# Scoring the second token tile beside the first, with constants and the first tile loaded first

## The chip, the cores and the metric

The kernel runs on one core of a Trainium2 chip. The metric is the device time of one execution in microseconds (us); lower is better. Engines: PE (TensorE, matrix products), DVE (VectorE), ACT (ScalarE), POOL (GpSimd, here the issuer of the gathers), SP (SyncE, the issuer of the plain loads and stores), and 16 DMA engines that move the data of both issuers.

## What is computed

An input of 2048 tokens of width 448 is normed; the result is the input plus two branches that both read the norm.

```python
x = A_q
xn = _layernorm(x, axis=-1)
return x + _A_ref(xn, A_k, A_v, A_shift_k, A_ssm_k, A_ssm_D) + _B_ref(xn, B_w_q, B_k1, B_k2, B_u, B_v)
```

Branch A is a short convolution of k (4 taps), times v, then a causal convolution of length 2048 for each channel (by Fourier transforms), times the normed input. Branch B picks experts:

```python
q = jnp.einsum("nd,dhc->nhc", xf, w_q)          # 16 heads, 2 x 256
s1 = jnp.einsum("nhd,ed->nhe", q1, k1)          # 64 keys; s2 likewise
i1 = jnp.argsort(-s1, axis=-1)[..., :K]         # K = 2; i2 likewise
...
top_e = jnp.take_along_axis(eidx, ord2, axis=-1)   # 2 of the 4 pairs
g = _softmax(top_s, axis=-1)
act = _gelu(jnp.einsum("nd,nhkd->nhk", xf, u[top_e]))
out = jnp.einsum("nhk,nhk,nhkd->nd", g, act, v[top_e])
```

So each token reads 32 rows of u and 32 of v, and which rows is known only after scoring.

## The kernel before

**Tiles.** The tokens are 16 tiles of 128. `XA` holds all of them (loaded by `load_x`, normed in place by `norm`).

**Weights and scores.** `weights(h)`, for each of the 16 heads: SP loads 896 KB of w_q into one of four buffers (`wqb`); PE multiplies it with the keys (`pw`, L415); ACT copies the product (L418); PE turns it (`pt`, L424); ACT and DVE split it into a high and a low part (L431 to L437) in `WR`. A load waits until the product that read its buffer has run. `turn(T)` turns a token tile on PE and splits it into `xh` (ACT) and `xl` (DVE). `score(T, n)` makes the scores of four heads (11 matmuls, L477 to L481), then DVE finds maxima (L486) and their places (L493). `pick` selects the experts of these heads on DVE and ACT, spreads them over partitions by a product (`place`, L556), and ACT writes `idx` and `gat` (L562), eight slots of tiles. Tile 0 is scored and picked in turns of four heads while the weights come in; tile 1 by itself once they are all there, with one `pick` for its 16 heads; later tiles in pairs.

**Experts.** A tile has eight batches (128 in all), a batch four gathers on POOL (L586), each of 128 rows of u and v side by side (448 KB), into a ring of five batches. At most six gathers are on their way (`OUTSTANDING`). A gather needs the `idx` of its two batches' four heads. Then DVE multiplies with the spread token tile (L619), ACT sums (L625), POOL (from batch 104 on DVE) forms the coefficients (L632, L633), and PE adds up the values in `pv` (L638). `fold` takes the tile out. Where PE would sit idle inside a tile it runs small filling products (L1094).

**Convolution.** In two parts of 28 and 84 groups of channels: `conv_first` (in0, in1; loads `kvh`, taps L703, first transform L720), `conv_mid` (sp0, sp1; L767 to L817), `conv_last` (out0, out1; turning L858, copy to `zt` L860, last product L865, gate L876). All work in areas of one tile `S1`; before, out0's `zt` has a tile of its own. in1 needs the space of the scoring's tiles, so `switch` frees these after the last tile is scored and out0 is done; its first loads and taps work in `S1` and need not wait for that.

**Order.** Nothing runs in the order of the source. Each operation is given to a planner (`Plan.solve`) with a duration and a key; the planner walks through modelled time and takes, on each engine, the ready operation with the smallest key. `nb` is the earliest planned time. The engines then run the planned sequence in order, whatever the true times; a late load therefore holds all that was planned behind its user on that engine. `RANK` adds to the keys of each kind of operation a correction, given at four points and interpolated between. Plain loads leave SP in the order of their keys: before, kk, two heads' weights, x0, two more heads, c1 (the identity and other constants), then x1, x2 to 3, x4 to 9, x10 to 15 and the weights of the other heads. `join` makes later writers of an area wait for earlier users.

## Time and profile before

| | us |
|---|---|
| median of 3 runs | 909.22 (908.57 to 912.37) |
| the profiled execution | 899.54 |
| its span, first to last instruction | 897.6 |
| weights of the last head turned (last L425 on PE) | 70.3 |
| last score (L481) | 499.6 |
| first and last gather issued | 41.6, 871.5 |

The profiled execution is 9.7 us shorter than the median; all times of the trace belong to it. Busy time of an engine says little here by itself: the stages have different limits, and what counts is which wait ends last in each.

### The profile page before, as it was taken

The page shows a single profiled execution, that of the slowest core. Times are in us where ns is not written, and L with a number is a line of the kernel's source. Part 1 is how long each engine was busy: PE and PEld are TensorE (multiplying, and loading weights), DVE is VectorE, ACT ScalarE, POOL GpSimd, SP SyncE. Part 2 cuts the span into 40 slices and gives each one's busy share as a digit, 9 for nine tenths or more (in the row PEclk, how much of TensorE's full clock was granted, in tenths as well). Part 3 has the DMA queues.
Part 4 walks back from the last instruction along what each step waited for, and adds up shares of the span by engine and source line. Part 5 has one row for each costly group of instructions (what it writes and reads, how often), then busy time and mean ns, then how long its engine had stood idle before and what let it go on. Part 6 is the DMA issues. An engine that isn't in the chain of part 4 may idle for free.

```text
span 897.6 us, 15165 instructions
## 1 busy us (share of the span) xinstructions
PE 734.1 (82%) x4696; PEld 465.9 (52%) x4696; DVE 673.5 (75%) x1570; ACT 568.2 (63%) x1874; POOL 593.5 (66%) x740
## 2 busy tenths in 40 slices
PE   5988988898888889888797878787688887778776
PEld 2436756556555565556465645465343443345554
DVE  3568988887787878787887867758798897864454
ACT  2598664557565766566663675537798887764562
POOL 0157587886777767776777677757877776665550
PEclk9899999998999989998998989999999999997797
DMA  9898798888989999898889899988999999999885
GB/s 372 345 398 296 229 309 304 294 284 301 313 314 318 304 314 311 309 332 297 297 293 344 294 309 343 356 326 295 354 318 325 319 328 313 309 309 336 299 299 143
DMA packets 62586, 279.47 MB, mean 311 GB/s; under 512 B 14112, under 2 KB 23584, under 8 KB 62240
## 3 DMA queue, kind: packets, MB, share of 16 engines
q0 software_dynamic: 40960, 234.91, 75.2%
q1 hardware_dynamic: 21536, 43.49, 13.7%
q8 instruction: 39, 0.64, 0.3%
q14 instruction: 51, 0.42, 0.1%
HBM read 272.29 MB, written 6.08 MB: 310 GB/s over the span
## 4 chain that ended last, share of the span: by engine, by line
PE 49%; ACT 12%; issue 12%; DVE 9%; DMA 7%; POOL 7%; another core or an unknown queue 3%; DVEq 0%; POOLq 0%; SPq 0%; ACTq 0%
PE pv L638 9%; ACT ring L625 6%; POOL ring L586 5%; PE bank L477 4%; PE bank L720 4%; PE bank L478 3%; PE bank L479 3%; PE bank L814 3%; PE pv L1094 3%; PE bank L771 3%; DMA ring<-in_uv_dram,idx 3%; PE bank L865 2%; DVE ring L619 2%; DMA S<-in_kvh_dram 2%
## 5 line engine op out<-in xcount | busy, mean ns | idle before, releaser
L586 POOL DMA_INDIRECT ring<-in_uv_dram,idx x512 | 509.3, 995 | 270.6 <-issue 91.3
L625 ACT ACTIVATE ring<-ring 128x448 f32<-128x448 f32 x512 | 288.4, 567 | 49.8 <-DVE ring L619 30.5
L619 DVE TENSOR_TENSOR ring<-ring,xs 128x1792 f32<-128x1792 f32 x128 | 256.9, 2014 | 54.7 <-DMA ring<-in_uv_dram,idx 37.6
L638 PE MATMUL pv<-ring,cc 128*32 128x448 f32 x1024 | 136.4, 604 | 67.3 <-issue 36.5
L486 DVE MAX8 SC<-bank 128x8 f32<-128x64 f32 x512 | 118.5, 232 | 37.2 <-PE bank L481 10.0
L625 ACT ACTIVATION_READ_ACCUMULATOR ring<-ring 128x1 f32 x512 | 97.0, 189 | 0.0
L1094 PEld LDWEIGHTS pv<-c 128*128 128x128 f32 x596 | 80.3, 201 | 26.6 <-issue 25.5
L477 PE MATMUL bank<-WR,xh 128*128 128x512 f32 x192 | 84.4, 440 | 2.7 <-ACT R L724 1.0
L720 PE MATMUL bank<-c,S 128*64 128x132 f32 x896 | 68.1, 295 | 22.1 <-issue 7.0
L1094 PE MATMUL pv<-c 128*128 128x64 f32 x596 | 85.6, 285 | 0.0
L478 PE MATMUL bank<-WR,xh 128*128 128x512 f32 x192 | 78.1, 407 | 0.0
L638 PEld LDWEIGHTS pv<-ring,cc 128*32 128x32 f32 x1024 | 21.3, 112 | 108.3 <-issue 65.0
L479 PE MATMUL bank<-WR,xl 128*128 128x512 f32 x192 | 77.3, 403 | 0.0
L720 PEld LDWEIGHTS bank<-c,S 128*64 128x64 f32 x896 | 53.1, 143 | 45.3 <-issue 12.5
L771 PE MATMUL bank<-x1b,S 128*128 128x336 f32 x132 | 51.6, 505 | 10.8 <-DVE x1b L839 7.0
L724 ACT ACTIVATE x1b<-bank 128x264 f32<-128x264 f32 x84 | 30.8, 387 | 40.0 <-PE bank L720 29.7
L788 DVE TENSOR_TENSOR S<-bank,S 128x224 f32<-128x224 f32 (+1 forms) x66 | 40.5, 620 | 18.6 <-ACT S L782 13.4
L703 DVE TENSOR_TENSOR S<-S 128x1024 f32<-128x1024 f32 x28 | 34.9, 1245 | 25.7 <-PE bank L720 11.5
L493 DVE FIND_INDEX8 SC<-SC,bank 128x8 uint32<-128x256 f32 x128 | 52.5, 423 | 0.0
L477 PEld LDWEIGHTS bank<-WR,xh 128*128 128x128 f32 x192 | 37.9, 197 | 26.6 <-issue 11.5
L782 ACT ACTIVATE S<-bank 64x112 f32<-64x112 f32 x132 | 33.9, 257 | 21.8 <-PE bank L767 13.0
L632 POOL TENSOR_TENSOR cc<-sm,c 128x128 f32<-128x128 f32 x104 | 46.0, 442 | 2.2
(142 smaller groups left out, 1090.8 us busy)
## 6 DMA issues: line engine op xcount, KB each, us to landing
R<-in_wq_dram SPq DMA_DIRECT2D x16, 896.0 KB
S<-in_kvh_dram SPq DMA_DIRECT2D x28, 400.0 KB
ring<-in_uv_dram,idx POOLq DMA_INDIRECT x512
S<-in_fq_dram SPq DMA_DIRECT2D x32, 128.0 KB
XA<-in_x_dram SPq DMA_DIRECT2D x2, 1344.0 KB
out_dram<-fo SPq DMA_DIRECT2D x12, 224.0 KB
x1b<-out_dram SPq DMA_DIRECT2D x9, 224.0 KB
out_dram<-XA SPq DMA_DIRECT2D x2, 840.0 KB
```

The lines of the kernel that those rows point to most:

```text
L477: nc.tensor.matmul(o, xh[:, c, :], wh[:, c, ns], start=(c == 0), stop=False)
L478: nc.tensor.matmul(o, xh[:, c, :], wl[:, c, ns], start=False, stop=False)
L479: nc.tensor.matmul(o, xl[:, c, :], wh[:, c, ns], start=False, stop=False)
L486: nc.vector.max(mx[:, 8 * n + j, :] if safe else m2[:, m, 2 * j:2 * j + 8], bank[s.i][:, 64 * j:64 * j + 64])
L493: nc.vector.max_index(m4i[:, 2 * m + g, :], m2[:, m, 8 * g:8 * g + 8], bank[s.i][:, 256 * g:256 * g + 256])
L586: g = nc.gpsimd.indirect_dma_start(dst, None, uv, bass.IndirectOffsetOnAxis(ap=idx[:, T % 8, r, j:j + 1], axis=0)).ins
L619: op("DVE", dve(m * D), lambda: nc.vector.tensor_mul(U[:, :m, :], U[:, :m, :], xs[:, :m, :D]), r=["xs"], w=u[:m], key=k, name="prod")
L625: op("ACT", 0.575, lambda r=r: nc.scalar.activation(U[:, r, :], U[:, r, :], AF.Copy, accum_out=aw[:, r:r + 1]), w=[u[r], ("aw", b % 4, r)] ...
L638: v = nc.tensor.matmul(pv[32 * r:32 * r + 32, :D], cc[b % 3][:, r, :], ring[:, b % RING, r, D:], start=(j == 0), stop=(j == NB - 1), tile_ ...
L720: nc.tensor.matmul(o[64 * i:64 * i + 64, w * j:w * j + w], src, f1[:, i, :], start=True, stop=True, tile_position=(0, 64 * i))
L771: op("PE", 0.95 * n / 448 + 0.05, lambda t=t, sl=sl: nc.tensor.matmul(bank[sl.i][:, :n], fm, x1[p][:, :, q, t, :], start=True, stop=True), ...
L1094: nc.tensor.matmul(pv[:, D:], ident, c1[:, P:P + 512 - D], start=False, stop=False)
```

## The change

The scores of tile 1 are made four heads at a time, right after tile 0's of the same heads; its 16 heads are still picked at once, after tile 0's last. Tile 1's load, norm and turning move into the weights' loop at head 2. `xh` and `xl` exist twice, by the tile's parity. The loads of x4 to 15 get a name of their own and an earliest planned time of 14 and 26 us; c1 and x0 are loaded ahead of the weights by their keys. For the space, `zt` goes: out0 uses a part of `S1` (where in1's taps stand), a third buffer for part 1's spectra lies in `Y`, and the scratch of the dynamic DMAs is halved. in1's first users of `S1` now wait for out0's last (`ob`, `out_in`). All ranks are new, with seven points instead of four. `safe` is a second pass over everything, which runs only if the quick search for the places of the maxima found a wrong one.

```diff
 RANK = {
-    "DMAc1": (-1.0, 0.0, 8.0, 64.5), "DMAc2": (43.5, 4.0, 37.0, 128.5), "DMAfb@out1": (247.5, -85.5, 210.0, 115.5),
...
-    "SPkk": (-458.5, -422.5, -565.5, -452.0), "SPkvh@in0": (122.0, 127.5, 8.5, 122.0), "SPkvh@in1": (-9.0, -11.0, -11.0, -11.0),
-    "SPlate@out1": (-46.5, -46.5, -46.5, -57.0), "SPwq": (0.0, 0.0, 45.5, 0.0), "SPx": (6.0, 6.0, 19.5, 22.0), "bad": (178.0, 100.0, 62.0, 46.5),
...
+    "E": (-24.0, 27.0, 27.0, 27.0, 27.0, 132.0, 179.0), "SPc1": (0.0, 0.0, 0.0, -4.0, -4.0, -4.0, -4.0),
+    "SPkk": (-7.5, -7.5, -7.5, 0.0, 0.0, 10.0, 10.0), "SPkvh@in0": (-52.0, -42.0, -22.0, -22.0, -14.0, -14.0, -14.0),
+    "SPwq": (42.5, 42.5, 39.5, -3.0, 18.0, 19.0, 15.5), "SPx0": (-0.5, -0.5, -0.5, -0.5, -0.5, -0.5, -0.5),
+    "SPxm": (57.5, 37.5, 29.5, -30.0, -30.0, -21.0, -31.5), "bad": (46.0, 46.0, 46.0, 50.0, 46.0, 8.5, 4.5),
...
-    zt = ap.tile([P, 512], F32, name="zt")
-    xh = fp.tile([P, 4, P], F32R, name="xh")
-    xl = fp.tile([P, 4, P], F32R, name="xl")
+    xhs = [fp.tile([P, 4, P], F32R, name=f"xh{i}") for i in range(2)]
+    xls = [fp.tile([P, 4, P], F32R, name=f"xl{i}") for i in range(2)]
-        second["Y"] = sp.tile([P, 2, CH * 84], F32, name="Y")
+        second["Y"] = sp.tile([P, 3, CH * 84], F32, name="Y")
-    load_x(0, 1, 0)
+    load_x(0, 1, 0, "x0")
...
+    def halves_of(T):
+        return str(T % 2), xhs[T % 2], xls[T % 2]
...
-            z, zk = (S1[:, 512 * i:512 * i + 512], ("zt", i)) if p else (zt, "ob")
+            z, zk = (S1[:, 512 * i:512 * i + 512], ("zt", i)) if p else (S1[:, 1600:2112], "ob")
...
     for h in range(H):
         weights(h)
-        if h == 6:
+        if h == 2 and not safe:
+            load_x(1, 2, 12.0)
+            norm(1, 2, 14.0)
+            turn(1, 16.0)
+        if h == 6 and safe:
             load_x(1, 2, 16.0)
             load_x(2, 4, 36.0)
         if h % 4 == 3:
             n = h // 4
             score(0, n, 4.0 + 2.2 * h)
             pick(0, n, n + 1, 4.0 + 2.2 * h)
-    load_x(4, 10, 50.0)
-    load_x(10, NT, 80.0)
-    norm(1, 4, 40.0)
+            if not safe:
+                score(1, n, 6.0 + 2.2 * h, 1)
+    if not safe:
+        load_x(2, 4, 36.0)
+        pick(1, 4, 8, 44.0)
+    load_x(4, 10, 50.0, "xm", 14.0)
+    load_x(10, NT, 80.0, "xm", 26.0)
+    norm(1 if safe else 2, 4, 40.0)
...
-    for T in range(1, 4):
+    for T in range(1 if safe else 2, 4):
         scores(T)
...
-    join(s1_mid + ["S1"], s1_first)
+    join(s1_mid + ["S1", "ob", "out_in"], s1_first)
     conv_first("in1", (1,))
...
-    nc = bacc.Bacc("TRN2", target_bir_lowering=False, num_devices=1, dynamic_dma_scratch_size=4096)
+    nc = bacc.Bacc("TRN2", target_bir_lowering=False, num_devices=1, dynamic_dma_scratch_size=2048)
```

More of the change, by code (lines that the diff above doesn't have):

```diff
@@ L354, in one_pass, with load_x @@
     MB = 1e-6 * 4 * P
[L357 to L358 removed]
+    def load_x(a, b, key, name="x", nb=0.0):
+        load(XA[:, a:b, :], x[:, a:b], MB * D * (b - a), [("x", t) for t in range(a, b)], key, nb=nb, name=name)
     def norm(a, b, key, act_=False):
```

38 lines of the change are left out of this document (16 added, 22 removed), and 58 rows, old and new, of the table RANK.

## The prediction

> **What bounds the kernel now.** I read the page first, then the stages (busy time of each engine by window), then the gathers alone by the same windows, then the order of time on POOL, PE, ACT and SP at the start and around 516 us, and the chain's end. From the page, and from the list of who waited for whom:
>
> ```profile
> span 897.6 us, 15165 instructions
> PE 734.1 (82%) x4696; PEld 465.9 (52%) x4696; DVE 673.5 (75%) x1570; ACT 568.2 (63%) x1874; POOL 593.5 (66%) x740
> q0 software_dynamic: 40960, 234.91, 75.2%
> L586 POOL DMA_INDIRECT ring<-in_uv_dram,idx x512 | 509.3, 995 | 270.6 <-issue 91.3
> L477 PE MATMUL bank<-WR,xh 128*128 128x512 f32 x192 | 84.4, 440 | 2.7 <-ACT R L724 1.0
> ...
> POOL ring L586 <- ACT gat L562: 52.8, 4, 40.5
> POOL ring L586 <- remote: 15.7, 18, 2.3
> ```
>
> No engine is full: PE, the highest, is at 82%. The 512 gathers are the thread that runs through the span: they move 234.91 of the kernel's bytes and take 75.2% of the 16 DMA engines, and POOL does little else. Four of their waits, 52.8 us together, are for `gat`, that is for expert numbers that the scoring has not delivered. The stages (columns: busy us and instructions of PE, PEld, DVE, ACT, POOL; then granted clock, DMA share, GB/s), and below them the gathers alone:
>
> ```profile
> 0.00:30.00 30.00, 17.28 (x75) 6.93 (x77) 12.50 (x51) 7.77 (x17) 0.55 (x6) 0.89 0.95 383
> 30.00:60.00 30.00, 27.98 (x156) 14.27 (x153) 18.07 (x70) 25.50 (x85) 9.87 (x11) 1.00 0.91 360
> 60.00:84.00 24.00, 19.01 (x133) 11.96 (x135) 20.33 (x63) 22.49 (x81) 16.60 (x23) 1.00 0.95 352
> 84.00:104.00 20.00, 20.00 (x150) 14.61 (x143) 17.33 (x76) 10.73 (x41) 11.08 (x15) 1.00 0.69 224
> 200.00:300.00 100.00, 86.36 (x504) 60.07 (x503) 79.30 (x224) 63.05 (x229) 71.92 (x96) 0.93 0.91 314
> 520.00:600.00 80.00, 61.12 (x613) 41.21 (x610) 51.73 (x70) 44.25 (x145) 58.10 (x68) 0.91 0.94 341
> ...
> 84.00:104.00 20.00, 8.11 (x9) 1.00 0.69 224
> 200.00:300.00 100.00, 62.27 (x65) 0.93 0.91 314
> 400.00:477.00 77.00, 46.58 (x49) 0.89 0.89 297
> ```
>
> In the steady part DMA is at 0.91 and a gather goes out every 100/65 = 1.54 us. Between 84 and 104 us nine go out in 20 us, one per 2.2, with DMA at 0.69: a hole. What it waits for stands in the order of time on POOL, with the two `gat` writes of ACT that end its waits (start, us, engine, line; in brackets the idle time before and its releaser):
>
> ```profile
> 41.61 1.10 POOL L586 DMA_INDIRECT ring<-in_uv_dram,idx  x1 [40.53 <-ACT gat L562]
> 85.93 1.18 POOL L586 DMA_INDIRECT ring<-in_uv_dram,idx  x1
> 96.26 0.95 POOL L586 DMA_INDIRECT ring<-in_uv_dram,idx  x1 [0.30 <-issue]
> 103.80 0.95 POOL L586 DMA_INDIRECT ring<-in_uv_dram,idx  x1 [6.59 <-ACT gat L562]
> ...
> 84.95 0.17 ACT L562 ACTIVATE gat<-bank 128x8 f32<-128x8 f32 x1
> 103.43 0.19 ACT L562 ACTIVATE gat<-bank 128x32 f32<-128x32 f32 x1
> ```
>
> The first gather goes out at 41.61, the 25th (the last quarter of tile 0) at 85.93, the 32nd at 96.26, and the 33rd, tile 1's first, only at 103.80, right behind the `gat` of 103.43. So **the front is late by two things: the first score and tile 1's expert numbers.** Why the first score is late (order of time, and two sizes from the DMA issues):
>
> ```profile
> 4.37 4.21 SPq L348 DMA_DIRECT2D XA<-in_x_dram  x4
> 8.81 0.63 DVE L371 BATCH_NORM_STATS2 nw<-XA 128x6 f32<-128x448 f32 x1 [8.81 <-DMA XA<-in_x_dram]
> 13.44 0.52 ACT L418 ACTIVATE S<-bank 128x448 f32<-128x448 f32 x1
> 23.97 3.25 PE L415 MATMUL bank<-R 128*64 128x448 f32 x8 [3.14 <-DMA R<-in_wq_dram]
> 31.79 0.47 PE L477 MATMUL bank<-WR,xh 128*128 128x512 f32 x1
> 89.86 0.39 PE L477 MATMUL bank<-WR,xh 128*128 128x512 f32 x1
> 92.13 0.39 PE L481 MATMUL bank<-WR,xl 128*128 128x512 f32 x1
> ...
> R<-in_wq_dram SPq DMA_DIRECT2D x16, 896.0 KB
> XA<-in_x_dram SPq DMA_DIRECT2D x2, 1344.0 KB
> ```
>
> The four loads of x issued from 4.37 stand ahead of the fifth head's weights; two of them are 1344 KB. Head 4's product starts at 23.97 after a wait for its load, and on PE's in-order queue everything behind it waits too, up to the first score at 31.79. ACT's first copy of a weight product stands at 13.44, behind the norm of tile 0, whose data came at 8.81.
>
> **The change, part by part.** The sum is against the profiled execution: 899.54 us, span 897.6. The median of the runs shown is 909.22, 9.7 above it; I take the difference that comes out of the sum off that median.
>
> *Loads.* By the new keys kk, x0, c1, x1 and x2-3 go ahead of all weights, and x4-15 follows with planned times of at least 14 and 26 us. Two loads of 1344 KB are 2.75 MB; at the 383 GB/s of the first stage that is 7.2 us off the arrival of head 4. The first head comes later: the four small pieces, 1030 KB by the code's shapes, 2.8 us at that rate, but ACT then has the norm behind it. If PE's order stays stuck on head 4, the first score comes at 31.8 - 7.2 = 24.6; if it can go at the pace of the loads (896 KB is 2.4 us) it comes about 11 us earlier. I take 8: it is nearest to the row of 23.97. The loads moved pass the weights on SP's queue; tiles 2 and 3, the first to be normed after tile 1, have their own load ahead of them.
>
> *Tile 1 beside tile 0.* No work is added; four scores, the turning and the selection of tile 1 move from 82 to 103 us into the weights' phase. Three of the four scores now come before tile 0's last. One took 92.13 + 0.39 - 89.86 = 2.66 us of PE, so 3 x 2.66 = 8.0 stand ahead of tile 0's last quarter, where PE is already busy 27.98 of 30 us. The 8 earlier and the 8 more cancel: tile 0's last `gat` stays near 84, and gather 25 with it or a little earlier (I take 2, for the norm that no longer holds ACT). Behind it VectorE has tile 1's maxima, which cost it time wherever they are. Tile 1's last score follows by 2.66, so its `gat` comes some 8 us after tile 0's, at 92, and the eight gathers between (85.93 to 96.26) cover that. So the 33rd gather follows the 32nd at 1.25: the hole of 6.59 goes, and 2 with the earlier quarter, 8.6; and batches 0 to 5, which stand earlier by 8, leave their values and buffers out of the way. I take a **lead of 9 us** at gather 33.
>
> Can DMA carry it? Up to 104 us it moved 30 x 383 + 30 x 360 + 24 x 352 + 20 x 224 KB/us = 35.2 MB. In 95 us that is 371 GB/s, between the 383 and the 352 of the first three stages; at 352 throughout it would take 100 us and leave 4. So the lead is 4 to 11. The Trainium skill, DMA: Bandwidth & Descriptors, Specifications, gives about 358 GB/s as the HBM limit of one core; by it, an estimate, 35.2 MB take 98 us and the lead is 6. The 383 GB/s over the first 30 us show that this core is not held to it here.
>
> *Two buffers of turned tokens.* They save at most what scoring's first matmul waits in all, 2.7 us by its row; a loss has no place, the instructions are the same. I take 1 and put it into the lead's rounding.
>
> *Scratch of dynamic DMA halved.* At most 6 gathers are on their way by the code. Waits for landings cost 15.7 us; if the smaller scratch bit, they would show first: between 0 and 15.7 more. I take 0, since the limit of 6 is met first before and after. The Trainium skill, DMA: Bandwidth & Descriptors, on the descriptor swizzle, counts 9 descriptors of 16 bytes per engine and side for a DMA to 128 partitions; 2048 bytes would hold 14 such gathers, which gives 0 too.
>
> *out0's turned blocks move into S1.* This adds a wait: the first loads of in1 now come after the last product of out0. Around 516 us (PE's order of time, and the chain):
>
> ```profile
> 515.82 0.83 PE L865 MATMUL bank<-c,zt 128*128 128x64 f32 x6
> 516.70 0.67 PE L720 MATMUL bank<-c,S 128*64 128x132 f32 x8
> ...
> 477.51 6.96 DMA S<-in_kvh_dram
> 484.93 1.23 DVE S L703
> 623.57 6.78 DMA S<-in_kvh_dram
> ```
>
> Today in1's first block is loaded at 477.51 and ready long before; its first product follows out0's last at once. After, load and taps come in between: 6.96 + 1.23 = 8.2 us. Queued behind that load on SP are the next blocks and the stores. In that stage PE, DVE and POOL have room (61, 52 and 58 of 80 us), so gathers and batches go on, and only the convolution slides. Between 0 and 8.2; I take 2, since PE's row of 520 to 600 has 19 us idle to catch up in.
>
> *The order.* All ranks are new, so nothing after the front is the same sequence. Its nearest rows are two stages with the same kind of work: 1.54 us a gather (200 to 300) and 77/49 = 1.57 (400 to 477). Over 512 gathers 0.03 us are 15 us, either way. I take 0.
>
> What is late at the end:
>
> ```profile
> 871.52 0.95 POOL L586 DMA_INDIRECT ring<-in_uv_dram,idx  x1 [2.61 <-ACT S L860]
> 888.20 0.83 PE L657 MATMUL pv<-G,c 128*128 128x336 f32 x2 [1.01 <-DVE G L881]
> 890.64 0.34 SPq L677 DMA_DIRECT2D out_dram<-fo  x1
> ```
>
> The last gather goes out at 871.52, and the last fold waits for the convolution's G. Both ends stand close, so a lead counts only if gathers and convolution both have it; the convolution gets it through the scores, which must end before in1 may start. **Sum: -9 + 2 + 0 = -7 us**: 892.5 for this execution, 909.2 - 7 = 902 for the median.
>
> **The rivals.**
> - *The lead is eaten on the way* (no change). For it: from 200 to 300 us PE is busy 86 of 100 and DMA at 0.91, so a pipeline ahead of its scores may just wait for them; the 33rd gather would be 9 us earlier and the last one as late as now. Against it: nine-tenths of DMA and four-fifths of VectorE are not all. Time: -9 + 9 = 0, 909 (within 4).
> - *in1 starts late and nothing catches up* (slower). Place: 516 us. Price: the first block 8.2 and, as two loads used to be ahead, the second one's 6.78: 15. It decides once the first product of in1 comes over 13.5 us after out0's last, lead of 9 and 4.5 included, and DVE in sp1 cannot make it up. For it: the last fold waits for G. Against: the 19 us of idle PE. Time: 909 - 9 + 15 = 915.
> - *The loads do not do it*: the first score still waits for a load, because x1 and x2-3 now stand ahead of head 0; then tile 0's last quarter is 8 us later (the three scores) and only the hole goes. Time: +8 - 6.6 = +1.4 at gather 33, with in1's 2 about 912.
> - *The order alone is better*: by the 15 us above with the lead, 909 - 7 - 8 = 894 for half of it.
>
> **How the numbers follow.** Forecast, -5 to -10: 0.42. Better order beside it, below -10: 0.18. Lead eaten: 0.20. Late in1 or a worse order: 0.13. Loads: 0.07. A measurement of this kernel tells about 0.5% from no change, 4.5 us. So faster 0.60, same 0.23 (the eaten lead and half of the loads' case), slower 0.17. The likeliest is 902. The range goes down to 888 (the lead at 11 and two thirds of the order's gain) and up to 915 (late in1); what is left out on each side is about a tenth.
>
> **What would show it.** Right: the first gather near 34 us instead of 41.6; no `gat` wait before gather 33, which starts near 95; DMA above 0.9 from 84 to 104; the last gather at 862 to 866. Wrong: head 4's product still waits past 20 us; tile 0's last `gat` later than 88; more than 9 us between the last L865 of out0 and the first product of in1; or a pace over 1.57 us a gather between 200 and 477. More than 15.7 us of waits for landings would put it on the scratch.

## The result and the profile after

The change made the kernel slower: 916.22 us (median of 20 runs, 907.74 to 925.26) against 906.59 for the kernel before (20 runs on the same chip), a ratio of 1.0117 with a 95% interval of 1.0086 to 1.0147, so some 10.6 us. (Ratios leave out the runs that fell into a slower state of the chip, four of after's 20 here, so they differ a little from the quotient of the medians.) A second set, z0 below, on a chip where before took 898 us, gave 1.0126 (1.0083 to 1.0168). The prediction was 902.0, within 888 to 915.

The profiled execution of after took 918.07 us. It lies 18.5 us above before's, which was near the quick end of before's runs, so a difference of the two profiles overstates the change by some 8 us. Of after's page the span and the busy times, and of its list of who waited for whom two rows (sum in us, count, mean):

```profile
span 916.3 us, 15263 instructions
PE 748.1 (82%) x4724; PEld 478.5 (52%) x4724; DVE 676.4 (74%) x1587; ACT 568.9 (62%) x1874; POOL 595.7 (65%) x740
```

```profile
POOL ring L609 <- ACT gat L585: 59.6, 4, 40.7
POOL ring L609 <- remote: 16.2, 16, 2.0
```

The totals hardly differ. There are still four waits for `gat`, and they are 6.8 us longer, not shorter (59.6 against 52.8). The waits that the profile puts to `remote`, which the prediction reads as landings, are what they were (16.2 against 15.7). The same stages as before (columns as in the prediction):

```profile
0.00:30.00 30.00, 17.91 (x89) 7.85 (x90) 15.72 (x70) 13.41 (x32) 0.55 (x6) 1.00 0.91 344
30.00:60.00 30.00, 24.46 (x122) 13.48 (x120) 20.33 (x94) 24.22 (x81) 7.73 (x8) 0.94 0.97 392
60.00:84.00 24.00, 21.45 (x138) 12.65 (x139) 20.44 (x62) 23.07 (x75) 11.97 (x16) 1.00 0.66 216
84.00:104.00 20.00, 19.01 (x114) 13.80 (x113) 16.74 (x69) 9.76 (x35) 10.80 (x14) 0.91 0.58 200
200.00:300.00 100.00, 88.83 (x520) 60.12 (x521) 80.38 (x221) 64.50 (x236) 72.94 (x99) 0.93 0.90 310
```

From 60 to 84 us DMA fell from 0.95 to 0.66 and from 84 to 104 from 0.69 to 0.58: fewer gathers went out. From 200 us on the stage reads like before's. So the time is lost in the first 112 us. GpSimd's order of time there:

```profile
41.77 1.10 POOL L609 DMA_INDIRECT ring<-in_uv_dram,idx  x1 [40.68 <-ACT gat L585]
...
64.64 0.94 POOL L609 DMA_INDIRECT ring<-in_uv_dram,idx  x1 [11.53 <-ACT gat L585]
...
80.19 0.94 POOL L609 DMA_INDIRECT ring<-in_uv_dram,idx  x1 [3.99 <-ACT gat L585]
...
97.66 0.20 POOL L656 TENSOR_TENSOR sm<-sm,gat 128x4 f32<-128x4 f32 x1 [4.43 <-ACT sm L650]
...
101.70 0.99 POOL L609 DMA_INDIRECT ring<-in_uv_dram,idx  x1 [3.36 <-ACT gat L585]
...
110.59 0.96 POOL L609 DMA_INDIRECT ring<-in_uv_dram,idx  x1 [0.15 <-issue]
...
112.13 0.98 POOL L609 DMA_INDIRECT ring<-in_uv_dram,idx  x1 [0.16 <-issue]
```

These are gathers 1, 9, 17, 25 (the first of each quarter of tile 0), 32 and 33; between them a small GpSimd operation waits 4.43 us for ScalarE. Beside the others (starts in us, from the order of time on GpSimd; the last two rows are runs told of below, on other chips):

| | 1 | 9 | 17 | 25 | 32 | 33 | 512 |
|---|---|---|---|---|---|---|---|
| before | 41.61 | 57.24 | 70.80 | 85.93 | 96.26 | 103.80 | 871.52 |
| after | 41.77 | 64.64 | 80.19 | 101.70 | 110.59 | 112.13 | 889.59 |
| z0, after again | 43.08 | 65.88 | 81.28 | 102.59 | 111.45 | 113.00 | 885.16 |
| y0, before's order | 38.84 | 54.65 | 67.64 | 82.33 | 92.76 | 101.49 | 820.74 |

Read from left to right: the first gather is not earlier; each quarter of tile 0 falls further behind, 15.8 us by gather 25; then the hole in front of gather 33 is indeed gone (33 follows 32 by 1.54 us instead of 7.54), which gives 6.0 back. That leaves gather 33 8.3 us late, and the lag is never made up.

The first column flatters after: TensorE's granted clock was 0.89 in the first 30 us of before's profile and 1.00 in after's and y0's. Beside y0, which keeps before's order there, after's gathers 1, 9, 17, 25 and 33 are 2.9, 10.0, 12.6, 19.4 and 10.6 us late: at equal clock the first gather is late too.

### The profile page after: what moved, and what is told of

Same layout as the page of the kernel before. It is cut to its first block, busy times and chain, and to the rows that moved or that the text cites. A ratio compares the mean times of both kernels' runs of the same rounds, so it can differ in the third digit from the quotient of the medians.

```text
span 916.3 us, 15263 instructions
## 1 busy us (share of the span) xinstructions
PE 748.1 (82%) x4724; PEld 478.5 (52%) x4724; DVE 676.4 (74%) x1587; ACT 568.9 (62%) x1874; POOL 595.7 (65%) x740
## 4 chain that ended last, share of the span: by engine, by line
PE 46%; issue 13%; DVE 12%; POOL 11%; ACT 9%; DMA 4%; another core or an unknown queue 2%; SPq 0%; DVEq 0%; POOLq 0%; ACTq 0%
POOL ring L609 9%; PE pv L661 8%; PE bank L743 4%; ACT ring L648 4%; PE pv L1126 4%; PE bank L837 3%; DVE ring L642 3%; PE bank L500 3%; DVE SC L509 3%; PE bank L888 3%; PE bank L794 3%; PE bank L502 2%; PE bank L501 2%; DMA ring<-in_uv_dram,idx 2%
## 5 line engine op out<-in xcount | busy, mean ns | idle before, releaser
L661 PE MATMUL pv<-ring,cc 128*32 128x448 f32 x1024 | 137.1, 608 | 58.8 <-POOL cc L655 31.6
L1126 PEld LDWEIGHTS pv<-c 128*128 128x128 f32 x624 | 84.4, 204 | 27.5 <-issue 26.7
L1126 PE MATMUL pv<-c 128*128 128x64 f32 x624 | 90.7, 288 | 1.1 <-issue 1.0
L743 PE MATMUL bank<-c,S 128*64 128x132 f32 x896 | 72.9, 312 | 16.7 <-DVE xl L488 4.5
L500 PE MATMUL bank<-WR,xh 128*128 128x512 f32 x192 | 81.9, 427 | 3.4 <-DVE SC L516 1.7
L661 PEld LDWEIGHTS pv<-ring,cc 128*32 128x32 f32 x1024 | 22.4, 113 | 108.3 <-issue 54.6
L743 PEld LDWEIGHTS bank<-c,S 128*64 128x64 f32 x896 | 58.3, 154 | 36.4 <-issue 13.2
L501 PE MATMUL bank<-WR,xh 128*128 128x512 f32 x192 | 76.0, 396 | 0.0
L794 PE MATMUL bank<-x1b,S 128*128 128x336 f32 x132 | 51.7, 500 | 12.7 <-issue 6.2
L888 PE MATMUL bank<-c,S 128*128 128x64 f32 x224 | 39.4, 328 | 18.9 <-ACT S L883 17.4
L888 PEld LDWEIGHTS bank<-c,S 128*128 128x128 f32 x224 | 35.4, 237 | 34.5 <-ACT S L883 22.6
```

What stands on the lines that cost most here:

```text
L500: nc.tensor.matmul(o, xh[:, c, :], wh[:, c, ns], start=(c == 0), stop=False)
L501: nc.tensor.matmul(o, xh[:, c, :], wl[:, c, ns], start=False, stop=False)
L661: v = nc.tensor.matmul(pv[32 * r:32 * r + 32, :D], cc[b % 3][:, r, :], ring[:, b % RING, r, D:], start=(j == 0), stop=(j == NB - 1), tile_ ...
L743: nc.tensor.matmul(o[64 * i:64 * i + 64, w * j:w * j + w], src, f1[:, i, :], start=True, stop=True, tile_position=(0, 64 * i))
L794: op("PE", 0.95 * n / 448 + 0.05, lambda t=t, sl=sl: nc.tensor.matmul(bank[sl.i][:, :n], fm, x1[p][:, :, q, t, :], start=True, stop=True), ...
L888: nc.tensor.matmul(bank[s.i][:, 64 * j:64 * j + 64], z[:, P * (j - a):P * (j - a) + P], f3, start=True, stop=True)
```

## The experiments

The runs fell on several chips, and before took 905, 898 or 845 to 846 us on them. Each ratio is to before on the same chip. Gather times in the first 110 us depend little on the chip (x9 and z1 share the order up to 70 us: gathers 1, 9 and 17 at 38.14, 56.32, 68.39 and 37.76, 55.06, 68.88; after and z0, on two chips, lie within 1.3 us up to gather 33). Later ones do and aren't compared across chips, but for gather 33 in the last table.

"Moved" below means: the kernel's own plan is kept, some of its operations get another place in it (the number is the place in the plan, not a time of the chip), and the three PSUM banks are given out anew in the resulting order. A gather whose TensorE operation now comes later in the program is no longer held to it. Nothing else differs.

The theories, by the letters that the expectations use: (A) tile 1's scores and other work stand in front of tile 0's selection and placement on in-order queues; (B) the loads and the later first product make the front late; (C) the early norm and the turns cover each other, so that taking one away frees nothing; (N) the early norm.

**First questions, within after: the norm, TensorE's time, in1.** The change's order also has the statistics, Newton steps and normalisation of tiles 4 to 15 much earlier than before's. x1 moves them back, the statistics to places from 60 on, the rest behind tile 1's selection:

```diff
+ stats 5..16 -> 60.0, 63.4, ... ; newton 4 -> 104.3 ; xn 5..16 -> 108.0, 108.9, ...
```

> The changed kernel with its own order kept, but statistics, Newton steps and scaling of tiles 4 to 15 moved behind tile 1's selection on ACT and DVE, where the kernel before had them. Theory 'the order': the norm of tiles 4 to 15 stands between tile 0's scores and their selection (3.4 us on DVE ahead of the second selection, about 1.9 us a tile on ACT), and is a good part of the delay: gather 9 at 59 to 61 instead of 64.6, gather 25 at 94 to 97 instead of 101.7, ratio to before 1.005 to 1.009. Theory 'the turns': the delay is PE's and the PSUM banks' work on tile 1, whatever ACT and DVE do beside it: gather 25 moves by under 2 us, ratio stays near 1.012.

Measured: 1.0197 (1.0091 to 1.0302); gathers 9, 25 and 33 at 65.60, 107.86 and 120.00. By the gathers, moving it that late is worse than leaving it (the ratios' intervals overlap): the statistics then stand between ScalarE's steps for the third and fourth quarters, and from 84 to 104 us ScalarE is busy 17.40 us of 20, in after 9.76.

x2 leaves out ten of the eleven products of each of tile 1's first three scores, so tile 1's choice of experts is only rough:

```diff
+            if T == 1 and n < 3 and not safe:
+                nc.tensor.matmul(o, xh[:, 0, :], wh[:, 0, ns], start=True, stop=True)
+                return
```

> The changed kernel in its own order, but tile 1's first three scores are made by one product of eleven each, so that tile 1's experts are chosen from approximate scores; their maxima stay. It takes 3 x 10 x 0.23 = 7 us off PE ahead of tile 0's last quarter. Theory 'the turns, by PE time': gather 25 comes 6 to 7 us earlier (95) and the ratio falls to 1.004 to 1.007. Theory 'the turns, by the three PSUM banks and VectorE behind them' or 'the order': gather 25 moves by under 3 us and the ratio stays over 1.008.

Measured: 1.0197 (1.0104 to 1.0289); gathers 9, 25, 33 at 65.42, 102.76, 113.21, all up to 1.1 us behind after's; the 6 to 7 us earlier aren't there. It isn't a clean zero, for x2's granted clock was 0.85 from 30 to 45 us and after's 1.00: the weight product in front of tile 0's second score took 3.25 us (1.73 in after) and the score 1.0 us more, so some 2.5 us of gain may be hidden. **TensorE's time for the early scores is at most the lesser part of what makes the front late.**

x3 issues in1's first two loads ahead of out0, and x4 puts after's wait of in1 for out0 into before, which the planner then orders anew from there on:

```diff
+ x3 (after): the first two SPkvh@in1 -> 436.0
- x4 (before): join(s1_mid + ["S1"], s1_first)
+              join(s1_mid + ["S1", "ob", "out_in"], s1_first)
```

> The changed kernel in its own order, but SP issues in1's first two loads before out0, as the kernel before did; only the taps still wait for out0. Theory 'late in1': of the time from out0's last product to in1's first, most goes (6 to 7 us of load), and the ratio falls by 0.004 to 0.006. Theory 'the front': the lag is there at gather 65 already; in1 gives under 2 us, ratio 1.010 to 1.012.

> The kernel before, with the changed kernel's wait of in1's first users of S1 for out0's last product; the planner gives another order from there on, with the ranks of before. Theory 'late in1': slower by 4 to 9 us, ratio 1.004 to 1.010, the front as before. Theory 'the front': the wait is covered by gathers and batches, ratio 0.997 to 1.003.

Measured: x3 1.0114 (1.0021 to 1.0208), the change's own ratio; x4 1.004 (0.999 to 1.009). The wait of in1 costs nothing or little.

**The queues, within after.** x6, x7 and x8 move tile 0's placements ahead of other work on TensorE's queue, or tile 1's scores behind them:

```diff
+ x6: place 4, idx 4, gat 4 -> 89.1 ; score (2,0) -> 89.3
+ x7: x6 and scores (1,0), (1,1), (1,2), (1,3) -> 36.6, 59.9, 75.3, 89.2 (behind place 1, 2, 3, 4)
+ x8: x6 and scores (1,0) to (1,3) -> 89.2 to 89.23 (all behind place 4)
```

> After, with place, idx and gat of tile 0's last quarter moved on their queues to right behind E of that quarter, ahead of the first score of tile 2 and of two batches' last products; all else in after's order. In after E ended at 93.6 us and place ran at 100.9. Theory A (placements stand behind other tiles' work on the in-order TensorE queue): gather 25 at about 95 instead of 101.7, gather 33 at 107 to 109 instead of 112.1, and most of these 4 us kept to the end: 912 to 914. Rival B (the loads and the later first product make the front late, the queue's order does not): gather 33 still waits for tile 1's own selection at about 107 to 112, nothing is left of it by gather 65, and the time stays at 916 to 918.

> After, with tile 1's score of each quarter moved on the TensorE queue from beside tile 0's score to right behind the placement of tile 0's quarter (its MAX8 and index searches follow it), and tile 0's last placement ahead of tile 1's last score; all else in after's order. Theory A (tile 1's scores and searches stand in front of tile 0's selection): gathers 9, 17 and 25 start 3 to 7 us earlier than 64.6, 80.2 and 101.7; gather 33 at 108 to 113; the time 908 to 914. Rival B (loads and first product): gather 9 at 63 to 65 and gather 17 at 79 to 81 as in after, the time 916 to 920.

> After, with all four scores of tile 1 moved behind the placement of tile 0's last quarter, which undoes the turns and keeps the loads, buffers, ranks and the order of everything else. Theory A: tile 0's gathers come as early as before but for the later first product: gather 9 at 58 to 61, 17 at 72 to 75, 25 at 88 to 91, and the wait for tile 1's selection in front of gather 33 returns with 6 to 10 us, gather 33 at 108 to 114; the time 910 to 917. Rival B: gathers 9, 17 and 25 stay within 2 us of after's 64.6, 80.2 and 101.7, gather 33 comes at 120 or later, and the time is 922 to 928.

Measured: x6 1.0146 (1.0106 to 1.0186), gather 25 at 97.61, gather 33 at 109.91; x7 1.0357 (1.0276 to 1.0437), 119.05 and 131.62; x8 1.0325 (1.0252 to 1.0397), 111.02 and 123.86. x6 has gather 25 four us earlier and gather 33 two, as theory A has it in direction; but the ratio is no lower. In x8 tile 1's first two scores are out of the way, and gathers 9 and 17 (63.78, 78.82) still come within 1.4 us of after's. x7 and x8 went far the wrong way, and x8's order of time on GpSimd and ScalarE says why:

```profile
91.22 0.58 POOL L686 TENSOR_TENSOR cc<-sm,c 128x128 f32<-128x128 f32 x1
110.02 0.21 POOL L687 TENSOR_TENSOR sm<-sm,gat 128x4 f32<-128x4 f32 x1 [18.23 <-ACT sm L681]
```

```profile
92.71 0.17 ACT L616 ACTIVATE gat<-bank 128x8 f32<-128x8 f32 x1
106.82 0.60 ACT L517 ACTIVATE xh<-bank 128x512 fp32r<-128x512 f32 x1 [13.94 <-PE bank L534]
```

The expert numbers were there at 92.71, but ScalarE's next instruction, the turned copy of tile 3, had to wait 13.94 us for the moved scores of tile 1, whose buffer it takes. Behind it stood the sums and the gelu, and behind the gelu, on GpSimd, the coefficients and then gather 25. One moved instruction had stopped three engines.

x10 mends that, x11 puts only the norm back to where before has it, x12 does both, x13 puts the order of the loads back as well:

```diff
+ x10: x8 and px 4, xh 4, xl 4 (turning of tile 3) -> 103.0, 103.1, 103.2
+ x11: stats 5..16 -> 38.95 to 85.0 ; newton 4 -> 99.1 ; xn 5..16 -> 104.2 to 119.0
+ x12: x10 and x11
+ x13: x12 and wq 1, 2, x0, wq 3, 4 first, x4-9 and x10-15 -> 0.9, 0.95
```

> As x8 (after, tile 1's four scores behind the placement of tile 0's last quarter), but the turning of tile 3, which waits for tile 1's last score to free its buffer, is moved behind too, so that it does not stand on the ScalarE queue ahead of the sums of the running batches. Theory A (what stands ahead on an in-order queue): the 18.23 us wait of GpSimd for the gelu in x8 goes; gather 25 at 93 to 98. Theory C (the early norm and tile 1's scores cover each other: each alone already holds tile 0's second selection): gather 9 stays at 62 to 65, since VectorE still does the Newton steps in front of the second selection. Rival B (loads alone): gathers 9 and 17 as in after and 25 too. Time, as a ratio to before: 1.005 to 1.02.

> After, with statistics, Newton steps and normalisation of tiles 4 to 15 put back where before has them (statistics spread from 39 to 85, Newton behind tile 1's selection); turns and loads as in after. Theory C: alone it gives little, since tile 1's MAX8 still stand in front of the second selection: gather 9 at 61 to 65, 25 at 98 to 104, ratio 1.008 to 1.025. If the early norm alone is the cause (against x1): gather 9 at 57 to 59, 25 at 90 to 94, ratio 1.000 to 1.005.

> Both of x10 and x11: after with the norm put back and tile 1's scores behind tile 0's last placement; loads as in after. Theory C: gather 9 at 57 to 60, 17 at 71 to 75, 25 at 86 to 90, gather 33 at 104 to 108 with the wait for tile 1's selection back, ratio 0.998 to 1.008. Rival B (the later first product): gather 9 still above 61, 25 above 93.

> x12 with the order of the loads put back to before's as well (first weights first, tiles 4 to 15 ahead of the fifth head's). All three edits of the front are then undone within after's order of the rest. If the front is all there is to it: gathers 1, 9, 17, 25, 33 within 2 us of before's 41.6, 57.2, 70.8, 85.9, 103.8 and a ratio of 0.997 to 1.005. If the newly searched order behind gather 33 costs by itself, the front is before's and the ratio still 1.007 to 1.012. If the loads cost nothing, x13 is no faster than x12; by x9 it is 3 us later at gather 1.

Measured: ratios 1.0378 (1.0327 to 1.0430), 1.0290 (1.0239 to 1.0342), 1.0506 (1.0461 to 1.0551) and 1.0553 (1.0497 to 1.0610); gather 9 at 64.73, 62.91, 64.46, 65.11; gather 33 at 125.01, 117.34, 132.81, 132.82. Gather 9 lies in x10 and x11 where theory C has it. x10's gather 25 (98.65) lies just above theory A's 93 to 98, x11's (104.48) just above C's 98 to 104, and both ratios missed. In x12 gathers 9 and 25 (103.73) lie where rival B has them; but so they do in x13 (103.53), which puts the loads back, so B is not it either. Even with all three parts undone, gather 9 did not come back to 57. What took their place shows in x12's second quarter, on VectorE and on TensorE:

```profile
49.12 0.16 DVE L574 TENSOR_TENSOR SC<-SC 128x4 f32<-128x4 f32 x1
...
52.46 0.56 DVE L485 TENSOR_TENSOR WR<-bank,WR 128x384 fp32r<-128x384 f32 x1 [3.18 <-ACT WR L481]
...
54.26 0.18 DVE L578 TENSOR_TENSOR SC<-SC,c 128x16 f32<-128x16 uint32 x1
```

```profile
60.45 3.25 PE L464 MATMUL bank<-R 128*64 128x448 f32 x8 [4.69 <-DMA R<-in_wq_dram]
63.63 0.31 PE L610 MATMUL bank<-SC,c 128*32 128x16 f32 x8
```

Tile 0's selection breaks off at 49.28 and goes on at 54.26, behind the residuals of two heads' weights (two pairs of steps, the first at 52.46) for which VectorE waits 3.18 us; in before the same two steps follow each other at 50.11 and 50.19. Its last ScalarE step ended at 56.74, but its placement (L610) stood behind a weight product that waited 4.69 us for its load. From the first gather to the end of that ScalarE step before took 12.7 us and after 21.3, 8.6 more; x11 (norm put back) takes 2.1 of it away, x10 (scores moved) 2.6, x12 (both) 4.2. So in this stretch norm and turns each cost some 2 us and don't cover each other; the other 4.4 us are the rest of the order that was searched for after.

And in x12's order of time on GpSimd a new wait stands in front of gather 28:

```profile
121.23 0.95 POOL L640 DMA_INDIRECT ring<-in_uv_dram,idx  x1 [14.01 <-PE bank L535]
```

The program holds each gather to the TensorE operation that its plan has ending just ahead of it; behind the moved scores that hold became a wait of 14 us. The rest of after's order is built around the three parts, and **undoing a part inside a fixed order doesn't measure the part.** At gather 9 itself theory C is neither shown nor excluded by these four.

**One part alone, in before's own order.** x9 moves only the two large loads, y1 only the turns, n1 only the norm. y1 needs the second buffer and so the space that the change makes (out0's small buffer in `S1`, in1 behind out0, the halved scratch); y0 has all that with no order changed, as its control:

```diff
+ x9: x4-9 -> 9.6 (behind head 5's weights) ; x10-15 -> 22.0 (behind head 9's)
+ y0: z = S1[:, 1600:2112] ; xh1, xl1 for tile 1 ; taps of in1 after out0 ; scratch 2048
+ y1: y0 and px, xh, xl of tile 1 -> 24.41 to 25.98 ; scores (1,0), (1,1), (1,2), (1,3) -> 33.94, 39.985, 55.275, 78.431
+     their MAX8 and searches -> 36.95, 44.17, 59.46 (ahead of tile 0's next selection), 82.17 ; selection of tile 1 -> 82.2
+     gathers 33 to 40 -> 90.92 on ; gathers 33 to 48 not held to TensorE's pace
+ n1: stats 5..16 -> 20.0 to 40.9 ; newton 3 -> 44.17 (ahead of tile 0's second selection) ; xn 5..16 -> 45.0 to 56.0
```

> Before, with the two loads of x tiles 4 to 15 moved from ahead of the fifth head's weights to behind the sixth and the tenth, the rest in before's order: the prediction's step Loads alone. If the step holds, the product of head 4 comes about 7 us earlier, the first score at about 24 to 28 us instead of 31.8, the first gather at 34 to 38 instead of 41.6, and the time is 2 to 5 us below before's. If the opening is bound by other things (buffers of weights and the copies on ScalarE and VectorE), the first gather stays within 2 us of 41.6 and the time within 2 us of before's.

> The control of y1 and y2: before's order unchanged up to out0, with the second buffer for tile 1, out0's small buffer in the staging space, in1 behind out0 and the halved scratch space, but tile 1 still scored where before scores it. Gathers 1 to 33 within 1 us of before's 41.6 to 103.8; ratio 1.000 to 1.008 by x4's 1.004. If the scratch space or the buffers cost anything before gather 201, it shows here as a lag that grows from gather to gather.

> Before's order and loads, with the turns alone: a second buffer for tile 1's transposes, tile 1's first three scores directly beside tile 0's and their MAX8 and searches ahead of tile 0's next selection, as after has them; tile 1's selection right behind its last score, and the gathers of tile 1 not held to TensorE's pace; out0's small buffer lies in the staging space as in after, so in1 starts behind out0. Theory A (the turns make the front late): quarter by quarter 2 to 4 us later, gather 9 at 59 to 61, 17 at 75 to 79, 25 at 91 to 97, the hole in front of gather 33 gone, and gather 33 at 102 to 108: no gain, ratio 1.00 to 1.01. The prediction's own step (VectorE and TensorE have room for them): gather 25 at 86 to 89 and gather 33 at 96 to 98, ratio 0.990 to 0.997.

> Before's order with the early norm alone: statistics of tiles 4 to 15 on ScalarE from the first score on, the Newton steps on VectorE in front of tile 0's second selection, the normalisation behind it, as after has them. Theory N (norm makes the front late): gather 1 later by 1 to 3 us, gather 9 at 60 to 66 and all later quarters as much behind. If the turns are the cause alone: gathers 9, 17 and 25 within 2 us of 57.2, 70.8 and 85.9. The time follows the start of gather 33: 1:1.

> The changed kernel itself, beside the others on their chip. It serves as the measure: ratio to before 1.008 to 1.016; gather 33 some 8 us behind before's and the end as much or more.

Measured: x9 1.0016 (0.9968 to 1.0064); y0 0.9991 (0.9958 to 1.0025); y1 1.0172 (1.0107 to 1.0237); n1 1.0176 (1.0117 to 1.0235); z0 1.0126 (1.0083 to 1.0168).

*Loads.* TensorE's order of time in y0 (before's order) and x9, the product of head 4 and the first line of the first score:

```profile
23.92 1.72 PE L463 MATMUL bank<-R 128*64 128x448 f32 x8 [3.14 <-DMA R<-in_wq_dram]
...
29.02 0.48 PE L533 MATMUL bank<-WR,xh 128*128 128x512 f32 x1
```

```profile
21.70 1.72 PE L446 MATMUL bank<-R 128*64 128x448 f32 x8
23.93 1.72 PE L446 MATMUL bank<-R 128*64 128x448 f32 x8
28.29 0.50 PE L508 MATMUL bank<-WR,xh 128*128 128x512 f32 x1 [1.28 <-DVE WR L468]
```

The wait of 3.14 us for head 4's load is gone in x9, and its product is 2.2 us earlier, not 7.2. The first score gains 0.7 (1.1 in z1, which has the same loads and a granted clock of 1.00 there; x9's was 0.94): it now waits 1.28 us for VectorE's residual of a weight. Gather 1 comes at 38.14 against 38.84, but gather 9 at 56.32 against 54.65, where a later head's product waits 1.93 us for its load (53.04), and gather 33 at 103.22 against 101.49.

*Buffers, scratch, in1's wait.* y0 is no slower than before: they cost nothing that these runs can tell.

*Turns.* y1's gathers 1, 9, 17, 25 and 33 start at 43.76, 61.95, 77.34, 91.84 and 109.22; against y0 they are 4.9, 7.3, 9.7, 9.5 and 7.7 us late. The 4.9 of the first come from TensorE's queue: tile 1 is turned ahead of the first score (31.76 instead of 29.02), and tile 1's first score stands 2.70 us ahead of the placement. ScalarE's order of time, the five `gat` of y1, then the last of y0:

```profile
43.38 0.17 ACT L619 ACTIVATE gat<-bank 128x8 f32<-128x8 f32 x1
61.35 0.17 ACT L619 ACTIVATE gat<-bank 128x8 f32<-128x8 f32 x1
76.98 0.17 ACT L619 ACTIVATE gat<-bank 128x8 f32<-128x8 f32 x1
90.88 0.17 ACT L619 ACTIVATE gat<-bank 128x8 f32<-128x8 f32 x1
101.29 0.19 ACT L619 ACTIVATE gat<-bank 128x32 f32<-128x32 f32 x1
```

```profile
101.12 0.19 ACT L619 ACTIVATE gat<-bank 128x32 f32<-128x32 f32 x1
```

Each of the first four is 5 to 10 us later than in y0 (38.44, 54.18, 67.27, 81.95). The last, tile 1's, comes at 101.29, while y0 has it at 101.12: **with the turns, tile 1 is chosen no earlier, and tile 0 later.** The time, 1.8% over the control, holds more than that. Behind gather 25 y1 has two holes that after has not (GpSimd's and VectorE's order of time):

```profile
97.45 1.03 POOL L643 DMA_INDIRECT ring<-in_uv_dram,idx  x1 [0.16 <-issue]
103.52 0.20 POOL L690 TENSOR_TENSOR sm<-sm,gat 128x4 f32<-128x4 f32 x1 [5.03 <-ACT sm L684]
```

```profile
120.94 1.23 DVE L760 TENSOR_TENSOR S<-S 128x1024 f32<-128x1024 f32 x1 [12.47 <-remote]
```

In front of gather 30 tile 1's selection, which this edit moved forward, stands on ScalarE ahead of a batch's sums. In front of gather 41 there are 13.0 us in which VectorE waits for a step of the convolution. Gather 33 is 3.8 us ahead of z0's on the same chip (113.00), gather 65 2.2 behind it (171.89 and 169.65). So y1 shows that the turns alone make gather 25 9.5 us late; it doesn't give their price in time.

*Norm.* n1 is as slow, with gathers 1, 9 and 33 at 50.64, 73.06 and 121.73. It starts the statistics sooner than after does (after's first gather is at 41.77): TensorE waits 5.93 us for ScalarE's copy of a weight product (42.45). Its granted clock was 0.65 from 45 to 60 us, before's 1.00, so the later gathers hold that too. It shows that an early norm is dear on ScalarE, not what after's own costs.

**Can the hole be closed otherwise?** z1 uses no second buffer: before with x9's loads, tile 1 turned right behind tile 0's last score, its four MAX8 and the selection ahead of the products of batches 5 and 6. y2 has the second buffer, and puts tile 1's first score where TensorE waits for weights, the next two behind tile 0's last:

```diff
+ z1: px 2, xl 2 -> 70.23, 73.561 ; scores (1,0) to (1,3) -> 74.9, 77.5, 78.6, 78.7 ; place 4 -> 77.0 ; selection of tile 1 -> 82.2
+     prod 5, 6 -> 82.45, 82.46 ; their sums, gelu, val behind it ; gathers 33 to 40 -> 90.92 on ; 25 to 48 not held to pace
+ y2: y0's space, x9's loads ; scores (1,0), (1,1), (1,2), (1,3) -> 48.25, 70.23, 73.22, 78.431 ; place 2, 4 -> 48.20, 77.0
+     MAX8 of tile 1 -> 53.6, 77.0, 80.135, 82.17 ; selection -> 82.2 to 85.1 ; gathers as y1
```

> Before with the loads of x9 and nothing but another order between 70 and 105 us: tile 1 is turned directly behind tile 0's last score, tile 1's four MAX8 and its selection stand on VectorE ahead of the products of batches 5 and 6, whose sums, gelu, coefficients and last products stand behind tile 1's placement; gathers 25 to 48 are not held to TensorE's pace. If the hole in front of gather 33 is VectorE's work in front of the selection: the hole falls from 9.5 us to 2 to 5 us, gather 33 at 96 to 100 instead of 103.2, and the time 0.3 to 0.8 per cent below before's. If the moved products are late next (the ring's slots of gathers 37 to 44): gather 33 is early, gather 45 to 65 is not, ratio 0.998 to 1.004.

> As y1 (second buffer, early scores of tile 1), with the loads of x9, but tile 1's first score stands where TensorE waits for the weights of head 13, its second and third behind tile 0's last score where TensorE only runs fills, their MAX8 behind tile 0's own selections, and tile 0's second and fourth placements ahead of what they waited behind. If the turns are late only by where they stand: gathers 9, 17 and 25 at 52 to 56, 67 to 71 and 80 to 85, gather 33 at 96 to 100 right behind gather 32, and a ratio 0.4 to 0.8 per cent below y0's. If VectorE has no room for three MAX8 ahead of gather 33 at any place: gather 25 or gather 33 is as late as in x9 (83.1, 103.2), and the ratio is y0's or above.

Measured: z1 1.0079 (1.0041 to 1.0116), gathers 25, 32, 33 at 85.09, 93.90, 103.28; y2 1.0052 (1.0020 to 1.0084), gathers 9, 25, 32, 33 at 58.83, 87.07, 105.34, 106.59. In z1 the hole is as long as it was (9.4 us), since VectorE now waited 3.12, 2.42 and 1.86 us ahead of three MAX8, the first of them tile 0's; the profile puts the second wait to a score and the others to `remote`. In y2 tile 1's `gat` came at 98.65, 2.5 us ahead of y0's, and was not used until 106.59. TensorE's and GpSimd's order of time in y2:

```profile
98.04 0.45 PE L613 MATMUL bank<-SC,c 128*32 128x64 f32 x8 [7.99 <-ACT SC L605]
98.42 3.68 PE L1151 MATMUL pv<-c 128*128 128x64 f32 x16
102.03 1.72 PE L695 MATMUL pv<-ring,cc 128*32 128x448 f32 x8
```

```profile
97.04 0.41 POOL L689 TENSOR_TENSOR cc<-sm,c 128x128 f32<-128x128 f32 x1
104.06 0.98 POOL L643 DMA_INDIRECT ring<-in_uv_dram,idx  x1 [6.61 <-PE pv L695]
```

TensorE idled 7.99 us in front of tile 1's placement, with the last product of a batch (102.03) queued behind it, though its coefficients were there at 97.04. Gather 31 waited 6.61 us for that product: by the program it is held to it, and this edit had freed only gathers 33 to 48. So the hole of gather 33 moved to gather 31. Whether y2 gains with gathers 25 to 32 freed too, or with the product ahead of the placement, wasn't tried. No version beat both kernels.

## Why the prediction was wrong

By its own steps, against gather times of the profiles:

- **Loads**, first score 8 us earlier, first gather near 34: failed. After's first score came at 29.01, 2.8 before before's 31.79, and even that is mostly not the loads': in before's profile the clock granted in the first stage was 0.89, and head 4's product took 3.25 us there and 1.72 in y0, whose first score, in before's order, came at 29.02. The step took the wait in front of head 4 for the whole of the delay. In x9 the wait went and 0.7 was left (1.1 in z1), and no gain in time (1.0016). In after, moreover, x0, x1 and x2-3 stand ahead of the weights (TensorE's order of time in after, its first products; then before):

```profile
10.82 5.31 PE L433 MATMUL bank<-R 128*64 128x448 f32 x16 [10.82 <-DMA R<-in_wq_dram]
```

```profile
6.13 4.77 PE L415 MATMUL bank<-R 128*64 128x448 f32 x16 [6.13 <-DMA R<-in_wq_dram]
```

  The first head came 4.7 us later, where 2.8 was worked out.

- **Tile 1 beside tile 0**, a lead of 9 us at gather 33: this step failed most. It priced three early scores as 8.0 us of TensorE that would cancel against the loads. Gather 25 came 15.8 us later than before's instead of 2 earlier. TensorE's time was at most the lesser part of the price: x2 took 7 us of that away and no gather came earlier. What the step left out is what stands behind a score: MAX8 and searches (some 3 us of VectorE each), a bank held until they end, and tile 0's own selection queued behind them. After's second quarter in VectorE's order of time, and the second and fourth in TensorE's:

```profile
46.09 2.10 DVE L509 MAX8 SC<-bank 128x8 f32<-128x64 f32 x8 [2.39 <-PE bank L504]
...
51.92 2.10 DVE L509 MAX8 SC<-bank 128x8 f32<-128x64 f32 x8 [2.12 <-PE bank L433]
...
54.74 0.15 DVE L396 TENSOR_SCALAR nw<-mv 128x12 f32<-128x12 f32 x1
...
57.98 0.16 DVE L540 TENSOR_TENSOR SC<-SC 128x4 f32<-128x4 f32 x1
```

```profile
54.88 2.17 PE L433 MATMUL bank<-R 128*64 128x448 f32 x8 [2.65 <-DVE SC L516]
...
89.77 0.50 PE L500 MATMUL bank<-WR,xh 128*128 128x512 f32 x1 [0.99 <-DVE SC L516]
...
96.62 0.96 PE L661 MATMUL pv<-ring,cc 128*32 128x448 f32 x8
...
99.44 0.96 PE L661 MATMUL pv<-ring,cc 128*32 128x448 f32 x8
...
100.92 0.27 PE L579 MATMUL bank<-SC,c 128*32 128x16 f32 x8
```

  Tile 0's MAX8 starts at 46.09 and its searches end at 49.8, but its selection starts only at 57.98: tile 1's MAX8 and searches and then the Newton steps of twelve tiles stand between. TensorE meanwhile waits 2.65 us (54.88) for a bank that tile 1's score holds, and the next weights with it. The fourth quarter lost 6.4 us more (from gather 17 to 25, 21.51 us instead of 15.13): the ScalarE step ahead of its placement ended at 93.64, and the placement (L579) ran at 100.92, behind two scores and two batches' last products (L661). y1 shows it as a part by itself: the turns alone make gather 25 9.5 us late. How the whole lag divides stays open, for y1 and n1 hold more than their part. For the stretch from gather 1 to the second selection, x10 to x12 give 2.6 of 8.6 us to the turns, 2.1 to the early norm, 4.2 to both, and leave 4.4 with the rest of the searched order.
  Two things in this step held: tile 1's `gat` came 7.6 us behind tile 0's last (8 was worked out), and the hole of 6.59 in front of gather 33 went (at 1.25 us from gather to gather it was worth 6.29; 6.0 came back). But tile 1's `gat` came at 108.98, 5.6 later than before's 103.43 (in y1 no earlier than in y0): the hole was not filled by earlier numbers; tile 0's gathers came too late to leave one.

- **Two buffers, scratch**: 1 and 0 were taken; y0 has both at 0.9991, so 0 is right. For the scratch this agrees with the count of descriptors that the prediction drew from the Trainium skill, DMA: Bandwidth & Descriptors, on the descriptor swizzle (the page has it for one 1 MiB transfer; the 14 gathers are an estimate from it).

- **out0's blocks in S1**, 2 taken, 0 to 8.2: in after in1's first product came 5.7 us behind the end of out0's last (524.03 + 0.88 to 530.58), but by x3, x4 and y0 the end doesn't feel it.

- **The order**, 0 taken: from gather 33 to 512 before took 767.7 us, after 777.5 and z0 772.2; y1 and n1, with before's order there, took 774.1 (with its hole of 13.0) and 758.1. That scatter is as large as any difference, so nothing shows that the searched order is better or worse behind the front; inside the front, x12 shows that it holds tile 0's selection.

- **The rivals.** "The loads do not do it" was nearest: it had the quarter 8 us later and only the hole gone. It had 0.07, and its mechanism only in part: the first head did come later, but the first score no longer waits for a load (TensorE's last wait before it, 0.71 us at 28.60, is for ScalarE), and its 8 us, three scores of TensorE, are neither the size of the 15.8 measured nor their kind. "The lead is eaten" had a lead to eat, and there was none. "in1 starts late" is out by x4 and y0.

Its marks for being wrong did appear: head 4's product past 20 us (23.23, though it now waits 0.45 us for VectorE and for no load), and tile 0's last `gat` past 88 (101.33). One of its marks for being right appeared as well, no `gat` wait in front of gather 33, and by itself it meant nothing.

A lag of the front is on the whole not made up (start of gather 33, and the time as a ratio to before on the same chip; before itself at 101 to 104):

| run | gather 33 | ratio | run | gather 33 | ratio |
|---|---|---|---|---|---|
| y0 | 101.49 | 0.9991 | x3 | 113.51 | 1.0114 |
| x4 | 103.03 | 1.0040 | x11 | 117.34 | 1.0290 |
| x9 | 103.22 | 1.0016 | x1 | 120.00 | 1.0197 |
| z1 | 103.28 | 1.0079 | n1 | 121.73 | 1.0176 |
| y2 | 106.59 | 1.0052 | x8 | 123.86 | 1.0325 |
| y1 | 109.22 | 1.0172 | x10 | 125.01 | 1.0378 |
| x6 | 109.91 | 1.0146 | x7 | 131.62 | 1.0357 |
| after | 112.13 | 1.0117 | x12 | 132.81 | 1.0506 |
| z0 | 113.00 | 1.0126 | x13 | 132.82 | 1.0553 |
| x2 | 113.21 | 1.0197 | | | |

From y0 to x13 gather 33 is 31.3 us later and the ratio 0.056 higher, 47 us of 845: the lag, and half as much again. (x10, x12 and x13 have 14 to 15 us of it from the hold of gather 28.) z1 and y1 lie above the line and lose later: y1 by the hole in front of gather 41, z1 by one of 10.3 us at the same place and by gather 37, which waits 6.28 us for the last product of a batch that was moved back. n1 alone got some back: 20.2 us behind y0's gather 33, its time is 16 to 17 us longer.

## What to carry to other kernels

Price an early piece of work by everything that it puts ahead of the critical chain on each in-order queue, and by the buffers it holds, not by the time of its first engine: three scores priced by TensorE's time alone made tile 0's experts ten us late (y1), by what stood behind them on TensorE's and VectorE's queues and in three banks. A long wait in front of one load is not the length of the delay behind it; look for what would be late next, and compare stages only at the same granted clock. To measure a part of a change, put it alone into the order that was tuned without it, with a control that has its buffers; taking it out of an order that was built around it only measures how that order breaks.

## What the runs showed of the hardware

- TensorE's granted clock in the first 30 us differs between executions of the same order, and the front moves with it: 0.89 in before's profile, where head 4's product took 3.25 us, and 1.00 in y0, where it took 1.72; the first score came at 31.79 and 29.02. A profile of the start is to be read with its clock.

- Chips differ by 6 to 7% for this kernel (before 905 and 898 us on some, 845 on others), though not in the opening. In x9's profile, on one of the latter (columns as above):

```profile
0.00:30.00 30.00, 20.05 (x92) 9.38 (x93) 14.09 (x55) 11.64 (x25) 0.55 (x6) 0.94 0.96 383
200.00:300.00 100.00, 88.96 (x539) 60.31 (x539) 87.91 (x252) 70.50 (x258) 79.66 (x109) 0.97 0.94 340
```

  The first stage moves 383 GB/s, as on before's chip, but from 200 to 300 us it is 340 against 314. What makes that difference wasn't tried.

- In after a MAX8 starts at 51.92, 2.9 us after its score's last product ended at about 49.0; the profile names a weight product of TensorE that was queued behind the score. z1 shows the like (a MAX8 at 95.74, its score's last product ended at about 93.4; put to `remote`). Whether that wait is real or a matter of missing records stays open.
